# Holding A by distance first and group second in the front stage of a chunked RWKV-7 kernel

## The chip, the cores and the metric

The kernel runs on one NeuronCore of one Trainium2 chip, in one launch. The metric is the device time of one execution in microseconds (us); lower is better. The core's engines work side by side, each through its own queue in order: TensorE (PE; its weight loads are shown as PEld), VectorE (DVE), ScalarE (ACT), GpSimd (POOL) and SyncE (SP), the last two and ACT also issuing DMAs. They wait for each other by semaphores. SBUF and PSUM each have 128 partitions; what one partition holds is counted here in words of four bytes, and a word of PSUM in a partition is called a column.

## The reference

An RWKV-7 recurrence over 4 batches x 8 heads, 768 tokens and 40 channels a head, followed by an RMS norm and a SwiGLU feed-forward layer over the 3072 resulting tokens (320 wide, 1536 inside). All is fp32.

```python
for t in range(S):
    y[:, :, t] = np.einsum('bhd,bhde->bhe', rt, state)
    Sa = np.einsum('bhde,bhe->bhd', state, at)
    state_decay = state * wt[:, :, None, :] - np.einsum('bhd,bhe->bhde', Sa, bt)
    state = state_decay + np.einsum('bhd,bhe->bhde', vt, kt)
...
rms = np.sqrt(np.mean(x * x, axis=-1, keepdims=True) + 1e-06)
xn = x / rms * rms_g
g = xn @ w_gate
silu = g * (1.0 / (1.0 + np.exp(-g)))
val = xn @ w_val
return (silu * val @ w_out).astype(np.float32)
```

## The kernel before

**Tiles.** The tokens are cut into 24 chunks of 32 (`C`). For each chunk, `front(c)` transposes the inputs and builds the scores inside the chunk, `inverse(c)` (or `early_inverse(c)` for the first four) inverts the triangular system that they form, and `main(c)` carries the state over the chunk, makes the outputs y and normalises them. After each second chunk, `feed(g)` runs the feed-forward layer on 256 tokens. `front` runs two chunks ahead of `main`. 16 slots (`NI`) per partition half hold the 32 heads, so most tiles have 16 blocks a partition.

**Order.** Every operation is first recorded with `plan.add` by a small helper (`tt`, `where`, `copy`, `mm`, ...) and then issued in an order written out by hand in the table `ORDER`; a "-" in it is a filler matmul on TensorE (line 1017). The table `PAIRS` says which of three PSUM tiles (two times 512 columns each) each use of PSUM, a `plan.room()`, takes. Each engine works in the order in which its own operations are issued. Because the helpers issue them, the profile shows one line for all operations of a helper: L446 for the DVE's, L469 for ACT's copies, L488 for matmuls, L491 for transposes, L485 for DMAs. Operations are therefore told apart by their tiles.

**The score matrix.** LT holds, for each of the 16 blocks, the 32 x 32 matrix of scores between tokens s (partitions) and t (words). It is filled in parts. Scores between tokens of the same group of four (a chunk has 8 groups g, with tokens j = 0 to 3) are the near scores, at distance 1, 2 or 3. Scores of the further levels (l = 4, 8, 16) come from the loop of line 713 and the masks `msk`.

**A and the near scores.** A holds, a block, 56 columns, seven for each group: the transposed input `a` of the tokens j = 1, 2, 3 (distance 1), the products of two of these with w (distance 2), and one with w twice (distance 3). Before the change it has the shape `[P, NI, 8, 7]`: the group first, then the seven. On it work:

- ACT's copy at line 681, which takes the tokens 1 to 3 of each group from the transposed input in PSUM (`A<-ps` in the profile); the copy of line 682 takes the tokens 0 into Ab (`Ab<-ps`).
- Two DVE products with w (lines 690 and 691; `A<-A,T`, 256 and 128 elements a partition). w is held token by token in T (`Tl[1]`), so its elements of one j lie four words apart.
- 32 matmuls of line 693, which multiply K with A's 56 columns into one PSUM room (`ps<-A,K`).
- Three masked steps of DVE at line 698 (`copy_predicated`, `LT<-near,ps`), one for each distance: where the mask `near` is set, the score is copied from PSUM into LT. LT and `near` are held token by token; distance 1 takes the words 1 to 3 of each group of four, distance 2 the words 2 and 3, distance 3 the word 3: 384, 256 and 128 elements a partition. From PSUM they take three, two and one of each group's seven columns.
- Two DVE products at line 709 (`Ab<-A,T`, 192 elements), which take the column 0, 3 and 6 of every second group (one per distance) for the next level's Ab.

After all levels, four DMAs take LT to the DRAM tile sB, from which M is read for the inverse (lines 749 to 756).

Of the kernel before, what the change touches and what calls it, by code (L numbers as in the profile page):

```python
# [9 lines left out]
U32 = mybir.dt.uint32  # L10
# [7 lines left out]
P = 128  # L18
# [352 lines left out]
def kernel(  # L371
# [42 lines left out]
    NI = 2 * N  # L414
# [14 lines left out]
    MUL, ADD, SUB = ALU.mult, ALU.add, ALU.subtract  # L429
    half = lambda i: slice(i * 64, (i + 1) * 64)  # L430
    part = lambda i: slice(i * 64, i * 64 + D)
# [12 lines left out]
    def dve(kind, fn, o, *args):  # L444
        m = lambda at: [at(x) if isinstance(x, bass.AP) else x for x in args]
        plan.add("DVE", kind, lambda at: fn(at(o), *m(at)), [o], aps(*args))  # L446

    def tt(o, a, b, op):
        dve("tt", nc.vector.tensor_tensor, o, a, b, op)
# [10 lines left out]
    def where(o, m, a):  # L460
        dve("where", nc.vector.copy_predicated, o, m, a)
# [6 lines left out]
    def copy(o, a):  # L468
        plan.add("ACT", "copy", lambda at: nc.scalar.copy(at(o), at(a)), [o], [a])  # L469
# [17 lines left out]
    def mm(o, lhsT, rhs, start=True, stop=True):  # L487
        return o, lhsT, rhs, lambda at: nc.tensor.matmul(at(o), lhsT, rhs, start=start, stop=stop, skip_group_check=True)  # L488
# [4 lines left out]
    def pe(kind, steps, more=[]):  # L493
        def issue(at):
            for s in steps:
                s[3](at)
        plan.add("PE", kind, issue, [s[0] for s in steps] + more, [x for s in steps for x in s[1:3]])
# [25 lines left out]
    for p0, kt, src in ((0, 0, 0), (0, 1, P), (0, 2, 2 * P), (64, 2, 2 * P)):  # L523
        m = min(P, DM - src)
# [7 lines left out]
    near = const.tile([P, 3, C], FP32, name="near")  # L532
# [38 lines left out]
    whole = lambda t: t  # L571
# [9 lines left out]
    Sd_ = Turns(2, [P, NI * D], "Sd", whole)  # L581
    T_ = Turns(3, [P, NI * 63], "T")
    K_ = Turns(2, [P, NI, 2, C], "K")
    A_ = Turns(1, [P, NI, 8, 7], "A", whole)

    Ab_ = Turns(2, [P, NI, C + D], "Ab")
    for t in Ab_.tiles:
# [32 lines left out]
    each = [(n, i, o) for n in range(N) for i in range(2) for o in range(2)]  # L620
# [33 lines left out]
    def front(c):  # L654
# [5 lines left out]
        for i in range(2):  # L660
# [6 lines left out]
            for x in range(2):  # L667
                at = i * 64 + x * C
# [5 lines left out]
        o = 0  # L674
        for l in LEVELS + (32,):
            Tl[l] = Tt[:, o:o + NI * C // l].rearrange("p (n t) -> p n t", n=NI)
            o += NI * C // l
        copy(by_i(Tl[1]), ps[:, :, :, 0])
        A, Ab = A_.next(), Ab_.next()
        a4 = ps[:, :, :, 1].rearrange("p n i t -> p (n i) t")  # L680
        copy(A[:, :, :, 0:3], a4.rearrange("p n (g j) -> p n g j", j=4)[:, :, :, 1:4])
        copy(Ab[:, :, 0:C].rearrange("p n (b h j) -> p n b h j", b=2, j=4)[:, :, :, :, 0], a4.rearrange("p n (h b j) -> p n b h j", b=2, j=4)[:, :, :, :, 0])
        K = K_.next()
        copy(K.rearrange("p (n i) x s -> p n i (x s)", n=N), turned(kb.rearrange("p n o e -> p n (o e)"), slot).rearrange("p n (i s) -> p n i s", i=2))
        LT = z["LT"] = LT_.next()
        z["KN"] = {1: flat(kb).rearrange("p a e -> p (a e)"), 2: KN_[2].next()}
        tt(z["KN"][2][:, 0:NI * D].rearrange("p (a e) -> p a e", e=D), flat(kb)[:, :, 0:D], wn, MUL)
        w4 = Tl[1].rearrange("p n (g j) -> p n g j", j=4)
        t2 = Tl[2].rearrange("p n (g x) -> p n g x", x=2)
        tt(A[:, :, :, 3:5], A[:, :, :, 1:3], w4[:, :, :, 1:3], MUL)  # L690
        tt(A[:, :, :, 6], A[:, :, :, 4], w4[:, :, :, 1], MUL)
        gr = plan.room().rearrange("p o (n t) -> p o n t", n=N)
        pe("gramk", [mm(gr[half(i), o, n, 0:56], K[part(o), 2 * n + i].rearrange("p x s -> p (x s)"),
                        A[part(o), 2 * n + i].rearrange("p g j -> p (g j)")) for n, i, o in each])
        g4 = gr.rearrange("p o n t -> p (o n) t")[:, :, 0:56].rearrange("p n (g j) -> p n g j", j=7)
        for dist, at in ((1, 0), (2, 3), (3, 6)):
            m = 4 - dist
            where(LT.rearrange("p n (g j) -> p n g j", j=4)[:, :, :, dist:], near[:, dist - 1:dist].rearrange(
                "p u (g j) -> p u g j", j=4)[:, :, :, dist:].bitcast(U32).to_broadcast((P, NI, 8, m)), g4[:, :, :, at:at + m])
        K1 = K_.next()  # L700
        lr = lambda t: t.rearrange("p n x (g h) -> p n x h g", h=2)
        tt(lr(K1)[:, :, :, 0], lr(K)[:, :, :, 0], lr(Tl[1][:, :, None])[:, :, :, 1].to_broadcast((P, NI, 2, 16)), MUL)
# [3 lines left out]
            k4 = K1[:, :, x].rearrange("p n (g j) -> p n g j", j=4)[:, :, :, 0:2]  # L706
            tt(k4, k4, t2[:, :, :, 1, None].to_broadcast((P, NI, 8, 2)), MUL)
        for x in range(2):
            tt(Ab[:, :, 16 * x:16 * x + 16].rearrange("p n (h j) -> p n h j", j=4)[:, :, :, 1:4], A[:, :, x::2, 0::3],
               w4[:, :, x::2, 0:1].to_broadcast((P, NI, 4, 3)), MUL)  # L710
        tt(Tl[4], t2[:, :, :, 0], t2[:, :, :, 1], MUL)
        K, A = K1, Ab
        for j, l in list(enumerate(LEVELS))[2:]:
            G = C // (2 * l)
            gr = plan.room().rearrange("p o (n t) -> p o n t", n=N)
# [7 lines left out]
            t = Tl[l].rearrange("p n (g x) -> p n g x", x=2)  # L723
# [21 lines left out]
            K, A = K1, A1  # L745
# [262 lines left out]
    for c in range(-2, NCH):  # L1008
        if c >= 0:
            main(c)  # L1010
            if c % CG == CG - 1:
                feed(c // CG)
        if c + 2 < NCH:
            front(c + 2)
            (early_inverse if c + 2 < EARLY else inverse)(c + 2)
# [34 lines left out]
```

## Time and profile before

| | us |
|---|---|
| median of 3 runs | 1079.48 |
| lowest and highest run | 1078.9, 1083.66 |
| span of the profiled execution, first to last instruction | 1078.2 |

The profiled execution's own time is its span, 1078.2 us; what lies around it is seen only as the 1.3 us between it and the median of the runs. The page of the profile gives each engine's busy time and its share of the span. "PE po<-ident" at L1017 are the filler matmuls. In rows of groups, the columns after the bar are the busy time of all in us, the mean of one in ns, and the engine's idle time before them with what ended it. In rows by tile there are minimum, median and maximum in ns, first and last start in us, and the shapes. The chain of waits is followed back from the last instruction: at each step to what released it, or to the instruction before it on its engine. In rows of the timeline and the chain, the first number is the start in us and the second the duration in us.

### The profile page before, as it was taken

The numbers are of one execution on the slowest core, as the hardware profiler recorded it, in microseconds if no ns is written. First come the engines' busy times: TensorE is split into PE (matmuls) and PEld (weight loads), VectorE is DVE, ScalarE is ACT, GpSimd is POOL, SyncE is SP. The second block draws the span as 40 slices with busy tenths as digits, with TensorE's granted clock in tenths as the row PEclk, the third lists the DMA queues.
The fourth block names the chain that finished last, engine by engine and source line by source line (L and its number), as shares of the span: only waits on it lengthen the run. The fifth ranks groups of instructions, "written<-read, shape, count | busy, mean of one in ns | idle before, by whom it ended". The sixth has DMA issues, their size and how long they took to land. (4 is left out here: it accounts for less than half of the span.)

```text
span 1078.2 us, 53465 instructions
## 1 busy us (share of the span) xinstructions
PE 1010.2 (94%) x23406; PEld 828.3 (77%) x23406; DVE 834.2 (77%) x2861; ACT 462.2 (43%) x1043; POOL 309.0 (29%) x554
## 2 busy tenths in 40 slices
PE   6767899999999999999999999998999999999998
PEld 6766778777888787877788778887777887887776
DVE  7887879876868888887897888887788889797420
ACT  6845756643543433532443434433344344342211
POOL 9714404120532223241331331331332331200000
PEclk9778999999999999999999999999999999999999
DMA  9965448766564364574465654665545553744242
GB/s 180 196 155 123 73 106 220 213 127 177 124 142 122 99 150 116 144 145 120 96 152 133 146 126 112 142 142 123 126 106 110 134 150 90 162 109 123 77 140 86
DMA packets 172456, 143.34 MB, mean 133 GB/s; under 512 B 125504, under 2 KB 143872, under 8 KB 172224
## 3 DMA queue, kind: packets, MB, share of 16 engines
q1 hardware_dynamic: 153856, 116.96, 42.4%
q0 software_dynamic: 16192, 22.64, 12.2%
q8 instruction: 184, 3.01, 1.2%
q10 hardware_dynamic: 2176, 0.33, 0.2%
q14 instruction: 48, 0.39, 0.1%
HBM read 123.86 MB, written 15.99 MB: 130 GB/s over the span
## 5 line engine op out<-in xcount | busy, mean ns | idle before, releaser
L488 PE MATMUL ps<-xg,wf 128*128 128x256 f32 (+1 forms) x1728 | 355.2, 392 | 4.7 <-DVE xg L446 1.1
L488 PEld LDWEIGHTS ps<-xg,wf 128*128 128x128 f32 (+1 forms) x1728 | 261.6, 189 | 60.4 <-issue 16.9
L488 PE MATMUL po<-wf,hT 128*128 128x320 f32 x576 | 180.1, 445 | 0.1
L446 DVE TENSOR_TENSOR tmp<-Yi,M 128x60 f32<-128x60 f32 (+24 forms) x620 | 129.5, 209 | 19.7 <-DMA M<-sB 6.9
L446 DVE TENSOR_TENSOR Yi<-Yi,tmp 128x60 f32<-128x60 f32 (+24 forms) x620 | 130.2, 210 | 12.7 <-DVE ss L446 0.2
L466 ACT ACTIVATE sg<-ps 128x256 f32<-128x256 f32 x144 | 52.4, 383 | 192.4 <-PE ps L488 182.7
L488 PEld LDWEIGHTS po<-wf,hT 128*128 128x128 f32 x576 | 102.6, 191 | 34.0 <-issue 1.7
L485 POOL DMA_DIRECT2D VU<-in_v_dram x92 | 53.6, 587 | 234.2 <-PE ps L488 157.0
L446 DVE TENSOR_TENSOR hT<-ps,sg 128x256 f32<-128x256 f32 x144 | 59.0, 419 | 62.4 <-ACT sg L466 55.9
L469 ACT COPY KN<-ps 128x640 f32<-128x640 f32 x96 | 66.2, 691 | 76.6 <-PE ps L491 27.9
L488 PEld LDWEIGHTS ps<-Ab,K 40*64 40x64 f32 x4608 | 78.3, 139 | 26.4 <-issue 8.5
L446 DVE TENSOR_TENSOR K<-K,T 128x512 f32<-128x512 f32 (+1 forms) x192 | 93.3, 495 | 4.2 <-ACT K L469 2.1
L488 PE MATMUL ps<-Ab,K 40*64 40x56 f32 x4608 | 88.0, 225 | 8.8 <-ACT K L469 3.7
L485 POOL DMA_DIRECT2D kbn<-in_b_dram x92 | 53.4, 584 | 147.9 <-PE ps L488 147.0
L446 DVE TENSOR_TENSOR As<-ps,msi 128x256 f32<-128x256 f32 (+1 forms) x186 | 79.2, 475 | 18.3 <-PE ps L488 17.4
L469 ACT COPY K<-K 128x256 f32<-128x256 f32 (+1 forms) x168 | 71.8, 443 | 41.3 <-PE ps L488 20.3
L488 PEld LDWEIGHTS ps<-As,KN 128*40 128x40 f32 x3072 | 64.6, 122 | 15.1 <-issue 9.7
L485 POOL DMA_DIRECT2D wn<-in_w_dram x92 | 51.6, 565 | 83.7 <-DVE KN L446 34.7
L485 POOL DMA_DIRECT2D kbn<-in_k_dram x92 | 53.5, 585 | 73.8 <-PE ps L488 73.5
L488 PE MATMUL ps<-As,KN 128*40 128x32 f32 x3072 | 71.1, 203 | 3.7 <-issue 2.7
L446 DVE TENSOR_TENSOR y<-y,ps 128x256 f32<-128x256 f32 x119 | 49.9, 419 | 19.7 <-PE ps L488 17.6
L446 DVE COPY_PREDICATED LT<-near,ps 128x384 f32<-128x384 uint32 (+2 forms) x72 | 52.3, 727 | 3.6 <-PE ps L488 1.9
(133 smaller groups left out, 1544.5 us busy)
## 6 DMA issues: line engine op xcount, KB each, us to landing
wf<-sW SPq DMA_DIRECT2D x144, 480.0 KB, 4.3
M<-sB SPq DMA_DIRECT2D x80, 128.0 KB, 3.8
rn<-in_r_dram SPq DMA_DIRECT2D x24, 160.0 KB, 4.5
sW<-ex SPq DMA_DIRECT2D x16, 240.0 KB, 4.3
out_dram<-o SPq DMA_DIRECT2D x48, 80.0 KB, 3.9
kbn<-in_k_dram POOLq DMA_DIRECT2D x92, 40.0 KB, 3.5
kbn<-in_b_dram POOLq DMA_DIRECT2D x92, 40.0 KB, 3.3
wan<-in_a_dram POOLq DMA_DIRECT2D x46, 80.0 KB, 4.7
```

The costliest lines, as they stand in the source:

```text
L446: plan.add("DVE", kind, lambda at: fn(at(o), *m(at)), [o], aps(*args))
L466: plan.add("ACT", "act", lambda at: nc.scalar.activation(at(o), at(a), f, **kw), [o] + aps(acc), [a])
L469: plan.add("ACT", "copy", lambda at: nc.scalar.copy(at(o), at(a)), [o], [a])
L485: plan.add(by, "dma", lambda at: queue.dma_start(out=o, in_=i), [o], [i])
L488: return o, lhsT, rhs, lambda at: nc.tensor.matmul(at(o), lhsT, rhs, start=start, stop=stop, skip_group_check=True)
```

## The change

A gets the shape `[P, NI, 7, 8]`: the seven (which of the distances and tokens) first, then the 8 groups. In PSUM the 56 columns of a block then stand in the same order, so each distance's columns are neighbours: 24, 16 and 8 of them. All views of A, of w and of LT, `near` and Ab that meet it are walked with j outside and the group inside. LT, `near`, T and Ab themselves are held as before. The number of instructions, their element counts, their order on each engine and their waits are the same in both kernels; in the matmuls the order of A's 56 columns alone differs.

```diff
-    A_ = Turns(1, [P, NI, 8, 7], "A", whole)
+    A_ = Turns(1, [P, NI, 7, 8], "A", whole)
...
-        copy(A[:, :, :, 0:3], a4.rearrange("p n (g j) -> p n g j", j=4)[:, :, :, 1:4])
+        copy(A[:, :, 0:3], a4.rearrange("p n (g j) -> p n j g", j=4)[:, :, 1:4])
...
-        w4 = Tl[1].rearrange("p n (g j) -> p n g j", j=4)
         t2 = Tl[2].rearrange("p n (g x) -> p n g x", x=2)
-        tt(A[:, :, :, 3:5], A[:, :, :, 1:3], w4[:, :, :, 1:3], MUL)
-        tt(A[:, :, :, 6], A[:, :, :, 4], w4[:, :, :, 1], MUL)
+        w_j = Tl[1].rearrange("p n (g j) -> p n j g", j=4)
+        tt(A[:, :, 3:5], A[:, :, 1:3], w_j[:, :, 1:3], MUL)
+        tt(A[:, :, 6], A[:, :, 4], w_j[:, :, 1], MUL)
         gr = plan.room().rearrange("p o (n t) -> p o n t", n=N)
         pe("gramk", [mm(gr[half(i), o, n, 0:56], K[part(o), 2 * n + i].rearrange("p x s -> p (x s)"),
-                        A[part(o), 2 * n + i].rearrange("p g j -> p (g j)")) for n, i, o in each])
-        g4 = gr.rearrange("p o n t -> p (o n) t")[:, :, 0:56].rearrange("p n (g j) -> p n g j", j=7)
+                        A[part(o), 2 * n + i].rearrange("p j g -> p (j g)")) for n, i, o in each])
+        g4 = gr.rearrange("p o n t -> p (o n) t")[:, :, 0:56].rearrange("p n (j g) -> p n j g", g=8)
         for dist, at in ((1, 0), (2, 3), (3, 6)):
             m = 4 - dist
-            where(LT.rearrange("p n (g j) -> p n g j", j=4)[:, :, :, dist:], near[:, dist - 1:dist].rearrange(
-                "p u (g j) -> p u g j", j=4)[:, :, :, dist:].bitcast(U32).to_broadcast((P, NI, 8, m)), g4[:, :, :, at:at + m])
+            where(LT.rearrange("p n (g j) -> p n j g", j=4)[:, :, dist:], near[:, dist - 1:dist].rearrange(
+                "p u (g j) -> p u j g", j=4)[:, :, dist:].bitcast(U32).to_broadcast((P, NI, m, 8)), g4[:, :, at:at + m])
...
         for x in range(2):
-            tt(Ab[:, :, 16 * x:16 * x + 16].rearrange("p n (h j) -> p n h j", j=4)[:, :, :, 1:4], A[:, :, x::2, 0::3],
-               w4[:, :, x::2, 0:1].to_broadcast((P, NI, 4, 3)), MUL)
+            tt(Ab[:, :, 16 * x:16 * x + 16].rearrange("p n (h j) -> p n j h", j=4)[:, :, 1:4], A[:, :, 0::3, x::2],
+               w_j[:, :, 0:1, x::2].to_broadcast((P, NI, 3, 4)), MUL)
```

## The prediction

> **What bounds the kernel now.** The page's first part comes first: which engine has least idle time.
>
> ```profile
> span 1078.2 us, 53465 instructions
> PE 1010.2 (94%) x23406; PEld 828.3 (77%) x23406; DVE 834.2 (77%) x2861; ACT 462.2 (43%) x1043; POOL 309.0 (29%) x554
> ```
>
> PE is busy for 94% of the span, but not evenly, so I read the stretches (columns: from:to, length, then PE, PEld, DVE, ACT, POOL busy) and the filler matmuls of line 1017.
>
> ```profile
> 50.00:250.00 200.00, 174.41 (x4626) 147.22 (x4625) 157.73 (x513) 119.94 (x258) 55.75 (x100) 0.95 0.64 152
> 250.00:500.00 250.00, 242.75 (x5763) 197.92 (x5764) 204.74 (x718) 103.46 (x240) 72.11 (x123) 1.00 0.54 130
> 500.00:750.00 250.00, 243.19 (x5883) 198.12 (x5879) 210.62 (x748) 100.43 (x232) 77.78 (x134) 0.99 0.56 131
> L1017 PE MATMUL po<-ident x302: 273/275/582, 3.3 to 233.9; 128*128 128x128 f32 x151
> ```
>
> From 250 us on PE has 7 us of idle time in 250, and DVE 45 and 39 us: PE bounds this stage, and DVE has about a sixth of the time free. Before 234 us, 302 filler matmuls of some 0.275 us (83 us) count as PE work; there PE waits for others. So a dearer DVE step should be felt early in full, later in part; a cheaper one can return little later, since PE has almost nothing left to give.
>
> The chain of waits says how often DVE itself sets the end. It is listed back to 785 us.
>
> ```profile
> PE 17%; DVE 4%; issue 2%; DMA 1%; POOL 1%; ACT 1%; SPq 1%; DVEq 0%; ACTq 0%; POOLq 0%
> 785.13 0.67 DVE K L446 x2
> ...
> 905.44 0.66 DVE LT L446
> 906.12 0.74 DVE LT L446
> 907.30 0.64 DVE LT L446
> ...
> 937.14 0.73 DVE LT L446
> 937.89 0.74 DVE LT L446
> 938.65 0.72 DVE LT L446
> 939.44 0.81 PE ps L488 x64
> L446 DVE COPY_PREDICATED LT<-near,ps x12: 714/726/740, 821.8 to 938.7; 128x384 f32<-128x384 uint32 x4, 128x256 f32<-128x256 uint32 x4, 128x128 f32<-128x128 uint32 x4
> ```
>
> DVE holds 4% of the span, 43 us, in a chain 293 us long (785 to 1078): 15%. The last row, the near steps from 785 to 950, counts 12 of them, so four fronts; the steps of two of the four stand on the chain. Between 15% and 50%, then, I take one third of what a front's steps grow by as the part that reaches the end, and keep both for the range.
>
> **The change, part by part.** It adds and removes no instruction, no DMA and no wait, and each engine's order stays; only access patterns change. So every term is a duration, 24 times (one front for each chunk of 32 tokens).
>
> *The three masked steps.* The shapes of DVE's steps, kept apart (busy us, mean ns):
>
> ```profile
> L446 DVE COPY_PREDICATED LT<-near,ps 128x128 f32<-128x128 uint32 x24 | 17.5, 729 | 0.4
> L446 DVE COPY_PREDICATED LT<-near,ps 128x256 f32<-128x256 uint32 x24 | 17.4, 726 | 0.3
> L446 DVE COPY_PREDICATED LT<-near,ps 128x384 f32<-128x384 uint32 x24 | 17.4, 726 | 2.9 <-PE ps L488 1.9 <-DMA out_dram<-o 0.8
> L446 DVE COPY_PREDICATED LT<-msk,ps 128x256 f32<-128x256 uint32 x72 | 31.2, 433 | 13.8 <-PE ps L488 8.8 <-ACT KN L469 3.8
> L446 DVE TENSOR_TENSOR T<-T 128x256 f32<-128x256 f32 x24 | 10.1, 420 | 4.0 <-ACT T L469 3.9
> L446 DVE TENSOR_TENSOR T<-T 128x16 f32<-128x16 f32 x24 | 4.1, 169 | 0.1
> ```
>
> The T rows give (420 - 169) / 240 = 1.046 ns an element and 152 ns fixed. A masked step in runs of four or more costs 433 for 256 elements, 165 ns fixed. The near steps cost the same 727 ns for 128, 256 and 384 elements. What they share is 128 runs: (727 - 165) / 128 = 4.39 ns a run, whether it holds one, two or three elements. Three things lie in such runs: the PSUM columns (every seventh starts a group), and the mask `near` and the target LT, where each run lies in a row of four words of its own. Which of them sets 4.39?
>
> Against PSUM: in building As, DVE reads every second column (`1:C:2`; 24 of the 42 steps of 512) and pairs with gaps (48 of the 144 of 256) at full rate, and ACT's read of single columns four and eight apart adds little (the second row has min/median/max):
>
> ```profile
> L446 DVE TENSOR_TENSOR As<-ps,msi 128x512 f32<-128x512 f32 x42 | 28.4, 680 | 2.9 <-PE ps L488 2.9
> L446 DVE TENSOR_TENSOR As<-ps,msi x186: 402/416/692, 90.1 to 1017.4; 128x256 f32<-128x256 f32 x144, 128x512 f32<-128x512 f32 x42
> L446 DVE TENSOR_TENSOR As<-ps,msi 128x256 f32<-128x256 f32 x144 | 54.2, 415 | 15.5 <-PE ps L488 14.5 <-ACT As L472 0.8
> L469 ACT COPY Ab<-ps 128x128 f32<-128x128 f32 x24 | 9.6, 398 | 4.2 <-PE ps L491 4.2
> L469 ACT COPY M<-ps 128x128 f32<-128x128 f32 x8 | 2.2, 272 | 5.5 <-PE ps L488 4.3 <-DMA wf<-in_moe_w_out_dram 1.2
> ```
>
> No step on As takes more than 692 ns: 680 is 1.03 ns an element above the fixed 152, 415 is 1.03 too, and 398 against 272 is 0.98 ns more for each single column. Nothing here comes near 4.39. Also, runs of one, two and three at a step of seven cover unlike numbers of column pairs, yet cost the same; in `near` and LT they cover exactly 128 rows of four words each time. I take the SBUF side as what is paid for: 4.39 ns for each row of four words that a masked step touches in part. The change then multiplies it: with the group innermost, each element sits four words from the last, and 384, 256 and 128 rows are touched in turn: 165 + 384 x 4.39 = 1851, 165 + 256 x 4.39 = 1289, and 727. Sum 3867 against 2181: 1686 ns more a front.
>
> The other bound: if PSUM is what is paid for, the PSUM side is at full rate afterwards and LT and `near` are plain strided accesses. Their price has bounds from the steps on A:
>
> ```profile
> L446 DVE TENSOR_TENSOR A<-A,T 128x128 f32<-128x128 f32 x24 | 9.6, 398 | 0.2
> L446 DVE TENSOR_TENSOR A<-A,T 128x256 f32<-128x256 f32 x24 | 11.0, 460 | 3.5 <-ACT T L469 3.5
> L446 DVE TENSOR_TENSOR Ab<-A,T 128x192 f32<-128x192 f32 x48 | 20.9, 441 | 0.2
> ```
>
> The first has all three operands at steps of seven, seven and four words: (398 - 152) / 128 = 1.92 ns an element. At 1.92 the near steps would take 902, 657 and 411, sum 1970, 211 ns less; at 1.046, 567, 433 and 299, sum 1299, 882 ns less. Between +1686 and -882 I take the upper end, for the equal cost of the three.
>
> [...]
>
> *The steps on A.* After the change A is read and written in neighbouring words, or at a step of two for Ab, but `w_j` steps by four or eight words, and Ab's target by four. The 256-element step has only T strided: between 420 and 152 + 256 x 1.92 = 644; the middle, 532, is 72 more. The 128-element one, between 285 (152 + 128 x 1.046) and 398: 342, 56 less. The two on Ab have target and T strided at every element, like the 398 row: 152 + 192 x 1.92 = 521, 80 more each (lower bound 353). Sum +176 ns a front, bounds -329 and +346.
>
> *ACT's copy into A.* It wrote runs of three and read runs of three; now it reads single columns four apart and writes neighbouring words.
>
> ```profile
> L469 ACT COPY A<-ps 128x384 f32<-128x384 f32 x24 | 13.9, 581 | 3.4 <-PE ps L491 3.4
> L466 ACT ACTIVATE sg<-ps 128x256 f32<-128x256 f32 x144 | 52.4, 383 | 192.4 <-PE ps L488 182.7 <-DVE hT L446 4.7 <-DVE Yi L446 3.5
> ```
>
> From 272 at 128 and 383 at 256, ACT's neighbouring columns cost 0.87 ns, so 384 would be 494. With 0.98 for each single, 870. I take 870, since the read is like that of Ab<-ps: +289, lower bound -87.
>
> *What is late next.* Behind the near steps DVE's queue holds work of three other stages:
>
> ```profile
> 937.14 2.24 DVE L446 COPY_PREDICATED LT<-near,ps 128x384 f32<-128x384 uint32 x3
> 939.00 0.42 DVE L446 TENSOR_TENSOR tmp<-Yi,M 128x63 f32<-128x63 f32 x1
> 939.29 0.41 DVE L446 TENSOR_TENSOR K<-K,T 128x256 f32<-128x256 f32 x1
> 939.43 0.79 PE L488 MATMUL ps<-Xs,LT 32*32 32x40 f32 x64
> ```
>
> The inverse (tmp, Yi) waits, K for the next gramk, hT for PE's out matmuls, and the PSUM room that the near scores occupy is held longer, for which PE's next user of that pair waits (939.43). ACT's KN copies and the DMAs from LT to sB follow the masked steps too.
>
> *Sum.* A front: 1.686 + 0.176 + 0.289 = 2.15 us; 24 of them 51.6 us; a third on the path 17.2 us. The profiled execution's span is 1078.2, so 1095.4; the median of the runs shown is 1.3 us over that span, and with it 1096.7: **1096 us**. With 15% it is 1087, with 50% 1105.
>
> **The rivals.**
> 1. *PSUM is what was paid for, and the gain is handed back* (not slower). Near steps 1970, A steps +176: DVE 35 ns less a front, ACT 289 more; 24 x 0.25 / 3 = 2 us: 1081 us. For it: no row has a DVE read of PSUM at a step of seven. Against: the rows at 1.03 ns.
> 2. *PSUM, and strided SBUF costs next to nothing* (faster). Near steps -882, A steps between -329 and +176, ACT between -87 and +289: a front 1.30 to 0.42 us less; times 24, a third of it: 10 to 3 us less, 1069 to 1076, say 1073. For it: a step of two words is free in the T rows. Against: the 398 row.
> 3. *PSUM, but a masked write at single words is dearer than the 398 row.* Midway between 1.92 and 4.39 ns, 3.15: 1375, 971, 568, sum 2914, 733 more; with +176 and +289, 1.20 us a front, 29 us, a third 10: 1089 us. It decides once a masked element costs more than about 2.2 ns, where the three together cost as much as now. [...]
>
> That the change does not do what it says is my forecast's core: the columns become neighbours, but they are not what is waited for.
>
> **How the numbers follow.** Chances: forecast 0.50, rival 1 0.17, rival 2 0.20, rival 3 0.13. Half a per cent, 5.4 us, is about what can be told from no change. Slower: 0.47 of the forecast, 0.03 of rival 1, 0.10 of rival 3: 0.60. Within: 0.03, 0.13, 0.05 and 0.03: 0.24. Faster: 0.15 of rival 2 and 0.01 of rival 1: 0.16. The forecast's own range is 1087 to 1105; the whole range must reach into rival 2: 1072 to 1106.
>
> **What would show it.** Steps of 1.85, 1.29 and 0.73 us confirm the forecast. The last is the test by itself: its mask and target do not change, its columns do. If it stays at 0.73, PSUM is cleared; if it falls to 0.3 or 0.4, the forecast is wrong, and the 384-element step then tells rivals 1 to 3 apart (0.9, 0.57, 1.4). A<-ps near 0.87 and Ab<-A,T near 0.52 test the small terms. If DVE grows by 45 us and the span by under 8 us, the third was wrong, and DVE's idle time took it.

## The result and the profile after

The changed kernel takes 1125.0 us (median of 6 runs, 1117.73 to 1131.72) against 1079.19 us (6 runs, 1075.61 to 1083.66). The ratio is 1.0392, with an interval of [1.0342, 1.0442]: slower by 37 to 48 us. The forecast had the sign; the time lies beyond its range.

First part of the page of the changed kernel, with the row of the chain's shares:

```profile
span 1129.5 us, 53465 instructions
PE 1037.0 (92%) x23406; PEld 851.1 (75%) x23406; DVE 883.6 (78%) x2861; ACT 460.7 (41%) x1043; POOL 310.7 (28%) x554
...
PE 55%; DVE 22%; DMA 9%; issue 5%; ACT 4%; POOL 3%; SPq 2%; DVEq 0%; ACTq 0%; POOLq 0%
```

The span is 51.3 us longer (the profiled execution is the slowest of the six; the medians lie 45.8 us apart). As 1129.5 - 1037.0 = 92.5 against 68.0, PE is idle for 24.5 us more; the other 26.8 us are PE *busy* for longer with the same 23,406 matmuls. DVE is busy for 49.4 us more. Groups by shape (busy us, mean ns, idle before) show where:

```profile
L446 DVE COPY_PREDICATED LT<-near,ps 128x384 f32<-128x384 uint32 x24 | 44.8, 1866 | 3.7 <-PE ps L488 2.9 <-DMA out_dram<-o 0.7
L446 DVE COPY_PREDICATED LT<-near,ps 128x256 f32<-128x256 uint32 x24 | 30.9, 1288 | 0.3
L446 DVE COPY_PREDICATED LT<-near,ps 128x128 f32<-128x128 uint32 x24 | 17.4, 725 | 0.4
L446 DVE TENSOR_TENSOR A<-A,T 128x256 f32<-128x256 f32 x24 | 15.0, 624 | 3.3 <-ACT T L469 3.2
L446 DVE TENSOR_TENSOR A<-A,T 128x128 f32<-128x128 f32 x24 | 9.4, 393 | 0.2
L446 DVE TENSOR_TENSOR Ab<-A,T 128x192 f32<-128x192 f32 x48 | 24.7, 522 | 0.2
L469 ACT COPY A<-ps 128x384 f32<-128x384 f32 x24 | 12.1, 502 | 3.4 <-PE ps L491 3.4
L488 PE MATMUL ps<-Ab,K 40*64 40x56 f32 x4608 | 91.0, 231 | 29.2 <-DVE K L446 8.0 <-DVE LT L446 6.1 <-DVE Yi L446 3.3
```

The near steps take 3879 ns a front for 2181, 1698 more; the steps on A 624 + 393 + 2 x 522 = 2061 for 1740, 321 more; ACT's copy 79 less. On DVE that is 2.02 us a front, 48.5 us in 24. The last row counts the gramk matmuls (the kernel's name for those that multiply K with A or Ab) of the levels after the first; the second gramk of a front, at l = 4, comes right behind the near scores. The same row before the change:

```profile
L488 PE MATMUL ps<-Ab,K 40*64 40x56 f32 x4608 | 88.0, 225 | 8.8 <-ACT K L469 3.7 <-issue 2.1 <-ACT ex L466 0.9
```

PE's idle time ahead of this one group rose from 8.8 to 29.2 us, 20.4 of the 24.5 us, and its releasers are now DVE's LT (the near steps), K and Yi behind them in DVE's queue. One front, the one numbered 16 from 0: before, in the timeline of PE, then after, in the chain and in the timeline (start us, us; in brackets the idle time before):

```profile
645.52 1.15 PE L488 MATMUL ps<-A,K 40*64 40x56 f32 x64
646.61 3.06 PE L488 MATMUL ps<-xg,wf 128*128 128x256 f32 x16
649.60 1.16 PE L488 MATMUL ps<-Ab,K 40*64 40x56 f32 x64
```

```profile
682.82 1.88 DVE LT L446
684.70 0.12 DVE Ab L446
684.81 0.13 DVE tmp L446
684.94 1.20 DVE LT L446
686.13 0.04 DVE T L446
686.17 0.73 DVE LT L446
686.90 0.06 DVE Yi L446
686.96 3.07 PE ps L488 x72
```

```profile
682.30 3.06 PE L488 MATMUL ps<-xg,wf 128*128 128x256 f32 x16
686.95 1.15 PE L488 MATMUL ps<-Ab,K 40*64 40x56 f32 x64 [1.60 <-DVE Yi L446]
```

Before, 3.06 us of feed-forward matmuls lay between the first gramk, whose scores the near steps read, and the second. That was just enough: DVE's row of the third near step in this front,

```profile
648.48 0.73 DVE L446 COPY_PREDICATED LT<-near,ps 128x128 f32<-128x128 uint32 x1
```

ends at 649.21, 0.39 us ahead of the second gramk. Steps that grow by 1.70 us overrun that cover, and the chain now runs through all three of them.

`PAIRS` puts the near scores and the second gramk into the same PSUM tile in 14 of the 24 fronts, this one among them. In ten of these the changed kernel's second gramk starts 0.06 us after the third near step's end, where before there were 0.06 to 1.47 us between them. The 14 fronts hold 12.1 of the 21.8 us that PE now waits ahead of the second gramk; in the other ten fronts (9.7 us) it waits for other work, mostly for DVE's K (some 5.8 us).

The granted clock tells of the busy half (stretches: from:to, length, busy time of PE, PEld, DVE, ACT, POOL, then the clock):

```profile
50.00:250.00 200.00, 173.77 (x4386) 149.73 (x4385) 155.08 (x475) 113.23 (x240) 60.19 (x107) 0.86 0.62 145
823.70:840.80 17.10, 16.91 (x374) 14.08 (x368) 11.65 (x36) 5.28 (x11) 2.86 (x5) 0.50 0.26 56
```

The first stretch was at 0.95 before and is at 0.86; it issues 240 matmuls fewer in the same busy time. The second is one of the stretches in which the trace has the clock at half. It begins behind a wait of the second gramk of front 19, whose 64 matmuls then take 1.84 us and not 1.15 as in front 16:

```profile
823.49 1.84 PE L488 MATMUL ps<-Ab,K 40*64 40x56 f32 x64 [2.07 <-DVE LT L446]
```

Over the run:

```profile
core 0: 1129.5 us, clock 0.951
```

Before it was

```profile
core 0: 1078.2 us, clock 0.980
```

### The profile page after: what moved, and what is told of

It is laid out like the page before. It is cut to its first block, busy times and chain, and to the rows that moved or that the text cites. A ratio compares the mean times of both kernels' runs of the same rounds, so it can differ in the third digit from the quotient of the medians.

```text
span 1129.5 us, 53465 instructions
## 1 busy us (share of the span) xinstructions
PE 1037.0 (92%) x23406; PEld 851.1 (75%) x23406; DVE 883.6 (78%) x2861; ACT 460.7 (41%) x1043; POOL 310.7 (28%) x554
## 3 DMA queue, kind: packets, MB, share of 16 engines
q1 hardware_dynamic: 153856, 116.96, 40.3%
## 4 chain that ended last, share of the span: by engine, by line
PE 55%; DVE 22%; DMA 9%; issue 5%; ACT 4%; POOL 3%; SPq 2%; DVEq 0%; ACTq 0%; POOLq 0%
PE ps L488 39%; PE po L488 9%; DVE LT L446 7%; PE ps L491 7%; DVE tmp L446 3%; DVE K L446 2%; SPq L485 2%; DVE Yi L446 2%; DMA kbn<-in_k_dram 2%; POOL kbn L485 2%; DVE hT L446 1%; ACT K L469 1%; DVE y L446 1%; DVE Ab L446 1%; PE po L1017 1%
## 5 line engine op out<-in xcount | busy, mean ns | idle before, releaser
L488 PE MATMUL ps<-xg,wf 128*128 128x256 f32 (+1 forms) x1728 | 359.9, 396 | 8.8 <-DVE hT L446 2.0
L488 PEld LDWEIGHTS ps<-xg,wf 128*128 128x128 f32 (+1 forms) x1728 | 265.2, 192 | 65.7 <-issue 16.5
L446 DVE TENSOR_TENSOR Yi<-Yi,tmp 128x60 f32<-128x60 f32 (+24 forms) x620 | 131.2, 212 | 12.7 <-DVE ss L446 0.2
L488 PE MATMUL ps<-Ab,K 40*64 40x56 f32 x4608 | 91.0, 231 | 29.2 <-DVE K L446 8.0
L488 PEld LDWEIGHTS ps<-Ab,K 40*64 40x64 f32 x4608 | 81.2, 144 | 48.0 <-issue 17.3
L446 DVE COPY_PREDICATED LT<-near,ps 128x384 f32<-128x384 uint32 (+2 forms) x72 | 93.1, 1293 | 4.4 <-PE ps L488 2.9
L469 ACT COPY K<-K 128x256 f32<-128x256 f32 (+1 forms) x168 | 71.7, 443 | 54.8 <-DVE K L446 29.4
L488 PEld LDWEIGHTS ps<-As,KN 128*40 128x40 f32 x3072 | 68.6, 128 | 14.2 <-issue 9.8
L488 PE MATMUL ps<-As,KN 128*40 128x32 f32 x3072 | 74.9, 208 | 2.8 <-issue 2.1
```

## The experiments

Ratios are to the kernel before on the same chip, with 95% intervals.

### Which access the masked step pays for

**A by distance, steps walked by group.** On the changed kernel; only the walk goes back.

```diff
-            where(LT.rearrange("p n (g j) -> p n j g", j=4)[:, :, dist:], ..., g4[:, :, at:at + m])
+            where(LT.rearrange("p n (g j) -> p n g j", j=4)[:, :, :, dist:], ..., g4[:, :, at:at + m].rearrange("p n j g -> p n g j"))
```

> A by distance as in the changed kernel, but the three masked steps walk the group outside and j inside, as before: LT and near in 128 runs again, PSUM columns eight apart inside a run. Row theory (a masked step pays some 4.39 ns for each row of four words that it touches in part, whatever PSUM is like): all three steps at 727 ns. PSUM theory: 384, 256 and 128 single columns, so 1.85, 1.29 and a third step apart from 727. The A steps stay as in the changed kernel (sum 2.06 us a front against 1.74) and ACT's copy at 0.50. Time, if the near steps carry the loss: 24 x 0.32 us = 8 us more DVE work, 1081 to 1087 us. If the A steps at the head of the front carry it: above 1105 us.

**Old A, steps walked by distance.** On the kernel before: the other half of the change.

```diff
-            where(LT.rearrange("p n (g j) -> p n g j", j=4)[:, :, :, dist:], ..., g4[:, :, :, at:at + m])
+            where(LT.rearrange("p n (g j) -> p n j g", j=4)[:, :, dist:], ..., g4[:, :, :, at:at + m].rearrange("p n g j -> p n j g"))
```

> A by group as before, and only the masked steps walk j outside and the group inside: PSUM columns seven apart, never neighbours, and each element in a row of its own in LT and near. Row theory: 1.87, 1.29 and 0.73 us as in the changed kernel. If neighbouring PSUM columns help at all, the first two are dearer than in the changed kernel. A steps as before (sum 1.74 us a front). Time, if the near steps carry the loss: 24 x 1.70 = 41 us more DVE work, 1112 to 1122 us. If the A steps carry it: below 1095 us.

**The mask alone.** In the changed kernel `near` is held with its words of one j as neighbours; in the kernel before it is held without gaps.

```diff
-                "p u (g j) -> p u j g", j=4)[:, :, dist:]...
+                "p u (j g) -> p u j g", j=4)[:, :, dist:]...
```

> The changed kernel with the mask held j first as well, so that the mask is read in neighbouring words and only LT is stepped by four. If the target's rows are what is paid for: 1.87, 1.29, 0.73 us and about 1120 to 1130 us, no change. If the mask's rows are: the steps fall to 0.57 to 0.90, 0.43 to 0.66 and 0.30 to 0.41 us, and the time to 1078 to 1090 us.

```diff
-            where(..., near[:, dist - 1:dist].rearrange("p u (g j) -> p u g j", j=4)[:, :, :, dist:]...
+            where(..., near[:, dist - 1:dist, 0:8 * m].rearrange("p u (g j) -> p u g j", j=m)...
```

> The kernel before with the mask held compact (24, 16 and 8 neighbouring words for the three distances); LT and PSUM are walked as before. If the target's rows are what is paid for: all three steps at 727 ns and 1076 to 1083 us. If the mask's rows are: about 0.57 to 0.70, 0.43 to 0.55 and 0.30 to 0.41 us, up to 0.9 us a front less, and 1060 to 1079 us, which would beat both kernels.

The 384-element step, in this order (A by distance and walked by group; old A walked by j; mask by j; mask without gaps):

```profile
L446 DVE COPY_PREDICATED LT<-near,ps 128x384 f32<-128x384 uint32 x24 | 17.4, 724 | 2.7 <-PE ps L488 1.9 <-DMA out_dram<-o 0.7
```

```profile
L446 DVE COPY_PREDICATED LT<-near,ps 128x384 f32<-128x384 uint32 x24 | 44.8, 1865 | 4.1 <-PE ps L488 3.0 <-DMA out_dram<-o 0.8
```

```profile
L446 DVE COPY_PREDICATED LT<-near,ps 128x384 f32<-128x384 uint32 x24 | 44.6, 1860 | 3.7 <-PE ps L488 2.8 <-DMA out_dram<-o 0.7
```

```profile
L446 DVE COPY_PREDICATED LT<-near,ps 128x384 f32<-128x384 uint32 x24 | 17.4, 725 | 2.9 <-PE ps L488 1.9 <-DMA out_dram<-o 0.8
```

| kernel | ratio |
|---|---|
| A by distance, walked by group | 1.0027 [0.9994, 1.0059] |
| old A, walked by j | 1.0374 [1.0333, 1.0416] |
| changed kernel, mask by j | 1.0372 [1.0293, 1.045] |
| kernel before, mask without gaps | 1.0021 [0.9983, 1.0058] |

Single PSUM columns eight apart cost what runs of three cost (first row); the new walk over the old PSUM layout costs what the whole change costs (second). The mask's layout changes nothing either way. So the target LT sets the price, and the loss is the walk's; the new A by itself costs nothing that can be told. The first kernel's time (1078.9 us) came out just below its range, the other three inside theirs.

**Probes behind the distance-3 step.** 128 elements each, 24 times, written over A.

```diff
+                lambda at, s=src: nc.vector.tensor_copy(wide, at(s)),
+                lambda at, s=src: nc.vector.tensor_tensor(wide, full, at(s), MUL),
+                lambda at, s=src: nc.vector.copy_predicated(tight, full.bitcast(U32), at(s)),
...
```

> The kernel before with five more DVE steps behind the step of distance 3, all on the same 128 columns of PSUM (step of seven), writing into the used-up tile A, so that what is computed after them is on other numbers. (a) a plain copy and (b) a product with the mask, both into single words four apart; (c) a masked step into neighbouring words; (d) a masked step into single words four apart with a mask of neighbouring words; (e) the same into every second word. If only a masked write pays by rows: (a) 0.28 to 0.40 us, (b) 0.28 to 0.41, (c) 0.29 to 0.41, (d) 0.73, (e) 0.45, since two words share a row of four. If it pays by each run, (e) is 0.73. If any write to single words four apart pays 4.39 ns, (a) and (b) are 0.73 as well.

The five groups (plain copy to every fourth word, product to the same, masked to neighbouring words, masked to every fourth word, masked to every second):

```profile
L713 DVE COPY_PREDICATED A<-near,ps 128x128 f32<-128x128 uint32 x24 | 17.4, 723 | 0.8
L714 DVE COPY_PREDICATED A<-near,ps 128x128 f32<-128x128 uint32 x24 | 15.5, 647 | 0.0
L710 DVE COPY A<-ps 128x128 f32<-128x128 f32 x24 | 14.8, 615 | 0.0
L711 DVE TENSOR_TENSOR A<-near,ps 128x128 f32<-128x128 f32 x24 | 9.3, 386 | 0.8
L712 DVE COPY_PREDICATED A<-near,ps 128x128 f32<-128x128 uint32 x24 | 9.0, 376 | 0.8
```

The same single words cost a product 386 ns and a masked step 723, which falls to 376 when its target's words are neighbours, with mask and PSUM columns still single. The plain copy's 615 comes from its place in line, and so does part of the 647 for every second word (both below). As it stands 647 met neither number expected, so a second set follows, again written over A:

```diff
+                lambda at, s=src: nc.vector.copy_predicated(to(4, 1), by(yes, 1), by(at(s), 1)),
+                lambda at, s=src: nc.vector.copy_predicated(to(7, 1), by(yes, 1), by(at(s), 1)),
+                lambda at, s=src: nc.vector.copy_predicated(to(4, 2), by(yes, 2), by(at(s), 2)),
+                lambda at, s=src: nc.vector.copy_predicated(to(6, 2), by(yes, 2), by(at(s), 2)),
+                lambda at, s=src: nc.vector.copy_predicated(to(8, 4), by(yes, 4), by(at(s), 4)),
+                lambda at, s=src: nc.vector.copy_predicated(to(8, 4, 1), by(yes, 4), by(at(s), 4)),
...
```

> The kernel before with nine more steps of 128 elements behind the step of distance 3, into the used-up tile A; what is computed after them is on other numbers. Masked, from eight neighbouring PSUM columns with a mask of neighbouring words, into: single words at a step of four, single words at a step of seven, pairs at a step of four, pairs at a step of six, fours at a step of eight from a full row, fours at a step of eight from one word later. If each run of fewer than four costs 4.39 ns: 0.73, 0.73, 0.45, 0.45, 0.30, 0.30 us. If each row of four that is touched in part does: 0.73, 0.73, 0.45, 0.45 to 0.59, 0.30, 0.45. Then a plain copy into single words at a step of four from PSUM (0.61 as in the first probes), the same from SBUF (0.61 if the target sets it, below 0.45 if PSUM does), and a masked step from SBUF (0.73 if the target sets it).

`to(step, run)` is L712 to L717 in the order of the diff; L718 is a plain copy from PSUM to every fourth word, L719 the same from SBUF, L720 a masked one from SBUF:

```profile
L712 DVE COPY_PREDICATED A<-near,ps 128x128 f32<-128x128 uint32 x24 | 22.9, 955 | 0.0
...
L720 DVE COPY_PREDICATED A<-near,K 128x128 f32<-128x128 uint32 x24 | 17.6, 735 | 0.8
...
L713 DVE COPY_PREDICATED A<-near,ps 128x128 f32<-128x128 uint32 x24 | 16.9, 706 | 0.8
...
L717 DVE COPY_PREDICATED A<-near,ps 128x128 f32<-128x128 uint32 x24 | 10.5, 440 | 0.8
L714 DVE COPY_PREDICATED A<-near,ps 128x128 f32<-128x128 uint32 x24 | 10.5, 439 | 0.8
L715 DVE COPY_PREDICATED A<-near,ps 128x128 f32<-128x128 uint32 x24 | 10.5, 437 | 0.8
L718 DVE COPY A<-ps 128x128 f32<-128x128 f32 x24 | 9.2, 382 | 0.8
L716 DVE COPY_PREDICATED A<-near,ps 128x128 f32<-128x128 uint32 x24 | 7.0, 292 | 0.8
L719 DVE COPY A<-K 128x128 f32<-128x128 f32 x24 | 7.0, 290 | 1.4
```

The first probe in line carries some 0.23 us that later ones don't: 955 here for what took 723 as the fourth of the first set; 615 there for what L718 does in 382 (PSUM columns seven apart there, neighbours here). Both have no idle time before them: their records start before the step ahead of them has ended and share some 0.38 us with it. The 647 of L714 in the first set is a third such record, and shares 0.37 us with L713:

```profile
516.68 0.72 DVE L713 COPY_PREDICATED A<-near,ps 128x128 f32<-128x128 uint32 x1
517.03 0.64 DVE L714 COPY_PREDICATED A<-near,ps 128x128 f32<-128x128 uint32 x1
```

Less the 0.23 us that the other two carry, it would be some 415 ns, an estimate that lies near the 0.45 us expected if two words in one row are paid once, and far from the 0.73 us of a price for each run.

With the forecast's 165 ns, and 4.39 ns for each row of four words that is touched, 64 rows should take 446: so do 64 pairs (439, 437), and so do 32 runs of four that start one word off and touch two rows each (440). 32 full rows take 292, near 165 + 32 x 4.39 = 305. So the unit is the row of four words; that two separate words in one row count once rests on the estimate alone.

### How much of added DVE time reaches the end

Work is issued twice or more in the kernel before. First the near steps, one of them and all three:

```diff
-            nc.vector.copy_predicated(at(o), at(m), at(a))
+            for _ in range(1 + again):
+                nc.vector.copy_predicated(at(o), at(m), at(a))
```

> The kernel before with the masked step of distance 1 issued twice: 0.73 us more DVE work a front at the place of the near steps, 17.4 us in all, nothing else. If what is added there reaches the end nearly in full (as 0.9 of the changed kernel's 49 us did): 1092 to 1098 us. If there is slack behind the near steps first: 1079 to 1086 us, with no wait at the second gramk matmuls of a front.

> The kernel before with all three masked steps issued twice: 2.18 us more a front at that place, 52 us in all. Path theory: like the changed kernel and somewhat beyond, 1120 to 1132 us, and the second gramk matmuls of the fronts wait 15 us or more in all (1.3 before). If the strided A steps or the changed layout had a share of their own: below 1112 us.

Then work elsewhere: `main`'s decay three times (`for _ in range(3)`), the masked steps of the later levels twice (again=1 on `msk`), the feed's hT product and the inverse's first tmp products twice:

```diff
+    def twice(o, a, b_, op):
+        def issue(*args):
+            for _ in range(2):
+                nc.vector.tensor_tensor(*args)
+        dve("tt", issue, o, a, b_, op)
...
-                tt(hTs[:, e], h[e][:, 1], sgs[:, e], MUL)
+                (twice if e == 0 else tt)(hTs[:, e], h[e][:, 1], sgs[:, e], MUL)
...
-            tt(tmp, Y[:, 0:n, i:i + 1].to_broadcast((P, n, m)), ...
+            (twice if i < 8 else tt)(tmp, Y[:, 0:n, i:i + 1].to_broadcast((P, n, m)), ...
```

> The kernel before with the product Sdec issued three times: 1.64 us more DVE work a chunk, 37.7 us in all, about as much as the masked steps grew by, but in the main stage. If DVE's total is what binds, or any DVE work on this queue reaches the end: 1108 to 1118 us, as with the masked steps. If the place in the queue decides: 1080 to 1095 us.

> The kernel before with the three masked steps of the further levels issued twice: 1.29 us more a front, 31 us in all, behind the second, third and fourth gramk. If the whole front is tight, as at the near steps: 1100 to 1112 us. If only the place ahead of the second gramk is: below 1095 us. If DVE's time is dear everywhere in the same measure, this and the next two cost alike.

> The kernel before with every second product hT issued twice: 1.26 us more a chunk, 30 us in all, in the feed-forward stage, just ahead of the out matmuls. If DVE's time is dear everywhere: 1100 to 1112 us. If the front is what is tight: 1080 to 1095 us.

> The kernel before with the first eight products of the inverse issued twice in 20 of the 24 chunks: some 0.2 us each, 33 us in all. If DVE's time is dear everywhere: 1100 to 1112 us. If the front is what is tight, and the inverse of a chunk has time in hand: 1080 to 1095 us.

Added DVE time is the profile's DVE busy less 834.2; the cost is the ratio's excess by the median before of the same chip; the last column is PE's idle time ahead of the later gramks, as in the rows of 8.8 and 29.2 (not given for the last dose).

| dose | DVE us added | ratio | cost us | share | idle |
|---|---|---|---|---|---|
| near step 1 twice | 16.6 | 1.0107 [1.0073, 1.0141] | 11.5 | 0.69 | 14.5 |
| all near steps twice | 51.8 | 1.0507 [1.0449, 1.0565] | 54.6 | 1.05 | 36.8 |
| old A, walked by j | 39.1 | 1.0374 [1.0333, 1.0416] | 40.3 | 1.03 | 25.0 |
| the change | 49.4 | 1.0392 [1.0342, 1.0442] | 42.3 | 0.86 | 29.2 |
| decay three times | 34.9 | 1.0188 [1.0124, 1.0251] | 20.3 | 0.58 | 11.1 |
| later masked steps twice | 29.4 | 1.0194 [1.012, 1.0268] | 20.9 | 0.71 | 10.4 |
| hT products twice | 28.9 | 1.0118 [1.0054, 1.0183] | 12.7 | 0.44 | 8.9 |
| inverse's products twice | 31.0 | 1.0202 [1.0112, 1.0291] | 21.8 | 0.70 | - |

No dose costs a third or less by its central value, but the ratios' intervals are wide: the share of the hT products lies between 0.20 and 0.68, that of the later masked steps between 0.44 and 0.98, so that places other than the near steps are hardly told apart. Near step 1 twice (1087.8 us) and the decay three times (1099.5) fell between their two ranges, and all near steps twice (1133.5) just above its own. Ahead of the second gramk a large dose costs all of itself, and only there does the idle time ahead of gramk grow much. The row of all near steps twice (in that kernel's numbering L463 is the masked steps' line):

```profile
L491 PE MATMUL ps<-Ab,K 40*64 40x56 f32 x4608 | 88.9, 229 | 36.8 <-DVE LT L463 8.2 <-DVE K L446 7.2 <-DVE Yi L446 6.4
```

What holds it is seen in the second set of probes, whose last read of PSUM is L718, with two probes on SBUF (L719, L720) behind:

```profile
L492 PE MATMUL ps<-Ab,K 40*64 40x56 f32 x4608 | 96.8, 241 | 60.3 <-DVE A L718 36.5 <-DVE K L446 7.4 <-DVE Ab L446 5.9
```

36.5 of 60.3 us ended with the last read of the near scores' PSUM room, not with the probes behind it, and all of these waits lie ahead of second gramks that use the same PSUM tile: in this kernel it is mostly that room which is waited for. 7.4 us ended with the K products further back in DVE's queue.

### Can PE use the gap

**Fillers in the gap.** On the changed kernel, 62 "-" in the order table ahead of the second gramk of 13 fronts, to hold the clock up while PE waits (here for two of them and in words):

```
front 0: ... [8 x -] gramk l=4 ...     front 1: ... [6 x -] gramk l=4 ...
```

> The changed kernel with 62 filler matmuls (17 us of PE work) put into PE's queue ahead of the second gramk matmuls of 13 fronts, where PE stood idle. Clock theory (PE's waits lower the granted clock, and the slower matmuls behind them are about half of the loss): half-clock stretches after 230 us become rare, the mean granted clock rises from 0.951 towards 0.98, and the time falls from 1125 to 1095 to 1112 us although PE does more. If the waits alone are the loss: 1122 to 1135 us.

Measured 1.0584 [1.0498, 1.067] (1138.5 us), slower than the change alone and above both ranges. The clock of the profiled execution is 0.964 against 0.951, but PE's busy time is 7 us more and the idle time of its gramk row is still 21.3 us: fillers took PE time from work that was late. The fillers are busy for 67.9 us in place of 51.0, so PE's other matmuls took 9.9 us less than in the changed kernel: at the better clock some of the busy time comes back, and the fillers cost more than that.

**Other work first.** On the changed kernel and on the kernel before, PE's next one or two pieces (feed-forward matmuls mostly) are issued ahead of the second gramk in 17 fronts, here for one of them and in words:

```
-  gramk l=4 (front 16), feed 6 h
+  feed 6 h, gramk l=4 (front 16)
```

> The changed kernel with the next one or two pieces of PE's work pulled ahead of the second gramk matmuls in 17 of the 24 fronts (where their needs allow it); nothing else. If the loss is that PE's fixed order puts a matmul right behind the near steps while other work is ready: the waits there fall from 20.6 us to below 10, and the time to 1095 to 1110 us. If DVE's total binds: 1120 us or more.

> The same order with the kernel before, as a control. PE hardly waited there (1.3 us), so the new order has little to give: 1075 to 1085 us. If it is below 1070, the order is better by itself, and the changed kernel's gain by it has to be read against this one.

Both missed: 1.076 [1.0659, 1.086] on the changed kernel, and 1.041 [1.0339, 1.0481] on the kernel before, as dear as the change itself, with no DVE work added (the second kernel, in a span of 1114.7 us):

```profile
PE 1028.7 (92%) x23406; PEld 840.2 (75%) x23406; DVE 832.5 (75%) x2861; ACT 461.2 (41%) x1043; POOL 309.4 (28%) x554
```

PE is given useful work instead of a wait, and the time is lost all the same: PE idle 86.0 us for 68.0, PE busy 18.5 us more (at a mean clock of 0.965 against 0.980). So a second gramk that comes *late* costs about as much as the change even when PE has other work meanwhile. The gramk of l = 8 behind it waits 9.1 us in all for 1.5 before. That the masks, ACT's copies and the feed work in DVE's and ACT's queues are placed for its old time too would account for the rest; no run takes this apart.

### A version that might gain

On the kernel before, the distance-1 step becomes a product of mask and score, since a product to the same words is cheaper (386 for 723 ns above):

```diff
+            if dist == 1:
+                tt(lt, mk.to_broadcast((P, NI, 8, m)), g4[:, :, :, at:at + m], MUL)
+            else:
+                where(lt, mk.bitcast(U32).to_broadcast((P, NI, 8, m)), g4[:, :, :, at:at + m])
```

> The kernel before with the step of distance 1 a product, mask times score, in place of the masked copy (what it writes as zeros is either zero already or written by later steps). A product showed 1.8 ns for single words and next to nothing for runs, so the step should fall from 0.73 to 0.56 to 0.65 us: 2 to 4 us of DVE work in all, just ahead of the second gramk. If time saved there is worth what small doses added there cost (0.7): 1074 to 1078 us beside 1078 for the kernel before, a gain at the edge of what can be told. If PE has nothing left to give: no difference.

```profile
L446 DVE TENSOR_TENSOR LT<-near,ps 128x384 f32<-128x384 f32 x24 | 13.1, 547 | 3.1 <-PE ps L488 2.1 <-DMA out_dram<-o 0.8
```

The step falls from 726 to 547 ns, 4.3 us in all; the ratio is 1.0004 [0.9975, 1.0034]. Time saved there gives nothing back that can be told (the interval leaves room for a gain of 2.7 us), while a large dose added costs all of itself. No kernel tried beats the one before.

## Why the prediction was right in sign and wrong in size

**What the masked step pays for: right.** Predicted 1851, 1289 and 727 ns, measured 1866, 1288 and 725. The test named in advance holds: the third step, whose columns become neighbours and whose target does not change, stays. Rivals 1 to 3 fall with it, as all rest on PSUM. The forecast spoke of "mask and target"; the mask's two experiments leave the target as the only one of the two that is paid for. Pairs of neighbouring words in the target do not bring the price of full rows: 128 elements take 439 ns in pairs at a step of four and 292 in full rows of four.

**The small terms.** The products on A were forecast at 532, 342 and 521 ns and took 624, 393 and 522: +321 ns a front for +176, inside the bound of +346 (its terms give 344). With T alone strided, in single words four apart, an element costs (624 - 152) / 256 = 1.84 ns, near the upper bound and not the middle. ACT's copy was forecast at 870 ns and took 502, at the lower bound of 494; I chose the wrong end, because the row of `Ab<-ps` has a strided target as well as a strided read, and I put its price on the read. The sum, 2.15 us a front (it adds ACT's time to DVE's as if both lay in one line), was measured at 1.698 + 0.321 - 0.079 = 1.94: 46.6 us for 51.6.

**The step that failed: "I take one third of what a front's steps grow by as the part that reaches the end".** The change's cost over its added DVE time is 0.86, the near steps' alone 1.03, the bounds were 0.15 and 0.50. With 0.86, the forecast's own 51.6 us would have given 1078.2 + 44.4 + 1.3 = 1124 us. The third came from the chain of waits, by how much of it was DVE and by two fronts of four. But the chain says who holds the end *now*; what a longer step adds to the waits is its growth less the slack ahead of whoever waits for it. That slack stood in the trace: 0.39 us in the front shown, against a growth of 1.70, and in the middle of the 14 fronts with a shared PSUM tile 0.36. Named in the forecast ("the PSUM room that the near scores occupy is held longer, for which PE's next user of that pair waits"), the wait was not sized.

**Left out altogether: the second half of the loss.** PE's busy time grew by 26.8 us in the profiled execution, and that is the clock. At half clock PE is busy for 100.0 us against 35.6 before, at full clock for 937.0 against 974.6; the 21,343 matmuls that have the full clock in both executions take the same time, within 0.7 us in all. With mean clocks of 0.980 and 0.951, and the half speed of the row of 0.50, (1 - 0.951) x 2 x 1129.5 = 111 us were at half clock against 43, 68 more, 36 of them (0.09 x 2 x 200) between 50 and 250 us. In the other five executions of the changed kernel the clock is 0.958 to 0.970, so there this part is smaller.

The waits of PE are short: the longest of all in the changed kernel is 3.3 us, ahead of the first filler (total us, times, longest):

```profile
PE po L1017 <- DVE po L519: 3.3, 1, 3.3
```

Between 250 us and the last instructions the clock halves five times, for 34 us in all, and each time a single wait of 1.5 to 2.1 us had begun 1.8 to 2.8 us earlier. Four of the five waits are those of a second gramk (fronts 10, 12, 19 and 20). So here the late gramk costs twice, once as a wait and once by the clock behind it. Not every such wait does this (one of 2.3 us at 989 us has no half clock behind it), and what decides is open.

A lower clock goes along with the loss (0.961 for the old A walked by j, 0.959 for all near steps twice, 0.965 for the kernel before with later gramks), but hT products twice cost 12.7 us at 0.979. What the change would cost at an unchanged clock stays open: the fillers meant to settle it took PE time themselves.

**A reading that was off.** The forecast counts 302 fillers of 0.275 us as 83 us of PE work. Their records overlap, and together they are busy for 47.3 us; no term rests on it.

**"PE has almost nothing left to give": not contradicted.** The product in place of the mask saves 4.3 us of DVE steps and gives no gain that can be told.

## What to carry to other kernels

In these runs a masked copy was priced by the rows of four words that its SBUF target touches (some 4.39 ns each, against 1.05 ns for an element): walk it so that each run fills whole rows, or as much of each as it can, before thinking of the PSUM side. In a kernel with a fixed order, the wait that a longer step makes is read front by front as its growth less the slack ahead of its first consumer on the bounding engine, and not from its share of the chain; look then for what the wait does to the clock behind it. The price has two sides: the step that just hid here gave nothing that can be told when it shrank, and took nearly all when it grew past its cover.

## What the runs showed of the hardware that was not expected

- A masked copy to single words costs nearly twice a product to the same words (723 against 386 ns at 128 elements), from PSUM and from SBUF alike (735); to full rows of four it takes 292, near the 152 + 128 x 1.046 = 286 of neighbouring words.
- ACT writes neighbouring words from single PSUM columns four apart in 502 ns at 384 elements, 79 ns less than runs of three into runs of three.
- A DVE record can start before the step ahead of it ends: three probes behind a masked step to single words began 0.35 us after it, shared some 0.38 us with it, and two of them read 0.23 us longer than their like later in line. Such a record is no price of its step.
- In the changed kernel, from 250 us on, the clock halved five times, for 3.4 to 17.1 us, behind single PE waits of 1.5 to 2.1 us.
